# Moving the streamed operands of a matmul 16 bytes further down in SBUF

## The chip, the cores and the metric

The kernel runs on 1 core of a Trainium2 chip. The metric is the device time of one execution in microseconds, over several runs of the same kernel on the same chip.

## What is computed

The reference is a windowed attention with a few sink positions, followed by a feed-forward layer with a leaky rectifier. All data is float32.

```python
# attention: B, H, S, D = 4, 8, 768, 64; n_sink = 4; window = 128
scores = scale * np.matmul(q, k.transpose(0, 1, 3, 2))
keep = is_sink | in_window                  # in_window: 0 <= i - j < window
scores = np.where(keep, scores, -1000000000.0)
a = softmax(scores)
attn = np.matmul(a, v)
x = attn.transpose(0, 2, 1, 3).reshape(B * S, H * D)     # 3072 x 512
# feed-forward: d_model 512, d_ff 2048
h = x @ w_in
g = np.maximum(h, 0.0) + alpha * np.minimum(h, 0.0)
out = g @ w_out
```

## The kernel before

The 3072 rows of x are cut into 12 chunks of 256 query positions. For each chunk the kernel first does the attention of all 8 heads (scores, softmax, values), which leaves x transposed: four slices of 128 model dimensions by 256 positions. Then comes the feed-forward part, in 16 slices f of 128 hidden units. While TensorE does the feed-forward slices of chunk c, the attention of chunk c+1 is threaded between them.

To get float32 accuracy from the fast matmul, each operand is split into a high and a low part: x into `xh` and `xl`, g into `gh` and `gl`, and each weight into two parts in the tile `w{f}` (8192 bytes a partition: input and output weights, high and low). A product is then three matmuls: high by high, high by low, low by high.

The first product, `gemm1` (line 894), takes for each slice f twelve matmuls: four slices of the model dimension times three part pairs. The weights `w` are the stationary operand (128 columns are loaded for each matmul), and x is the moving operand, 256 columns of 4 bytes. ScalarE and VectorE then make g from the result (lines 898 to 901) and split it. The second product, `gemm2` (lines 929 to 932), takes six matmuls per slice f: here `gh` or `gl` is the stationary operand and the weights `w` stream, 512 columns.

The weights of all 16 slices stay in SBUF. They are loaded and split during the first two chunks.

The order of the work is written down in `program` as a list of operations with costs and needs; a planner (`Plan.draw`) plays them through and fixes, for each engine, one order and, for each rotating buffer, which copy is used. The planner's costs are constants: it does not know addresses. So the order of instructions does not depend on where a tile lies.

A tile has the same byte offset in all 128 partitions. The allocation puts tiles one after the other. In the kernel before, 15 of the 16 weight tiles start 32 bytes beyond a multiple of 128, and `w14` starts 64 beyond one, since it comes ahead of the others, behind a tile of 64 bytes. The tiles of `xh`, `xl`, `g`, `gh` and `gl` start 96 bytes beyond a multiple of 128. All of these tiles, and all slices that a matmul takes from them, are multiples of 128 bytes long, so that for every matmul of line 894 the moving operand lies 64 bytes beyond the stationary one, modulo 128 (32 for f=14). The two buffers `kq` of the scores (lines 597 and 598) start at 96 and at 0.

Of the kernel before, what the change touches and what calls it, by code (L numbers as in the profile page):

```python
# [10 lines left out]
F32R = mybir.dt.float32r  # L11
# [8 lines left out]
P = 128  # L20
# [4 lines left out]
QC = 2 * P  # L25
# [4 lines left out]
KT = DM // P  # L30
LAG = 2
# [290 lines left out]
def program(ctx, tc, qk, pairs, vp, vq, vs, w, par, out):  # L322
    nc = tc.nc
    const = ctx.enter_context(tc.tile_pool(name="const", bufs=1))
    fast = ctx.enter_context(ExitStack())
    pool = fast.enter_context(tc.tile_pool(name="main", bufs=1))
    psum = ctx.enter_context(tc.tile_pool(name="psum", bufs=1, space=bass.MemoryType.PSUM))
    plan = Plan(tc)
# [6 lines left out]
    def several(name, n, shape, dtype):  # L335
        plan.kind(name, [pool.tile(shape, dtype, name=f"{name}{i}") for i in range(n)])
# [17 lines left out]
    several("sinkT", 1, [P, QC], F32R)  # L354
    several("vs", 1, [P, DM], F32R)
    several("ob", 2, [P, DM], F32)
    several("xh", 2, [P, KT, QC], F32R)
    several("xl", 2, [P, KT, QC], F32R)
    several("g", 2, [P, QC], F32)
    several("gh", LAG + 1, [P, QC], F32R)  # L360
    several("gl", LAG + 1, [P, QC], F32R)

    size = const.tile([P, NF], F32, name="size")
    sizes = held(size)
# [182 lines left out]
    xh, xl, prep, comb, sink, ptile_, sums, rinv, nms, wt = {}, {}, {}, {}, {}, {}, {}, {}, {}, {}  # L547
# [730 lines left out]
```

## Time and profile before

| what | before |
| --- | --- |
| median of 3 runs | 677.37 us (676.48 to 678.82) |
| span of the profiled execution | 676.2 us |
| TensorE (PE) busy | 663.8 us, 98% |
| VectorE (DVE) busy | 525.8 us, 78% |
| ScalarE (ACT) busy | 397.5 us, 59% |
| granted TensorE clock, mean | 0.994 |

The profiled execution's span, 676.2 us, is the time from its first to its last instruction; it stands 1.2 us below the median of the timed runs. In the profile, PE is the matmul stream and PEld is the loading of stationary operands, which runs beside it. The duration of a matmul contains a tail that the profiler models; the time that a matmul really costs in a stream is the distance from its start to the next start. The names in a row are tiles: `bank<-xh,w` is a matmul into a PSUM bank with moving operand xh and stationary operand w; `bank<-w,gh` has the weights moving and gh stationary.

### The profile page before, as it was taken

The page shows a single profiled execution, that of the slowest core. Times are in us where ns is not written, and L with a number is a line of the kernel's source. Part 1 is how long each engine was busy: PE and PEld are TensorE (multiplying, and loading weights), DVE is VectorE, ACT ScalarE, POOL GpSimd, SP SyncE. Part 2 cuts the span into 40 slices and gives each one's busy share as a digit, 9 for nine tenths or more (in the row PEclk, how much of TensorE's full clock was granted, in tenths as well). Part 3 has the DMA queues.
Part 4 walks back from the last instruction along what each step waited for, and adds up shares of the span by engine and source line. Part 5 has one row for each costly group of instructions (what it writes and reads, how often), then busy time and mean ns, then how long its engine had stood idle before and what let it go on. Part 6 is the DMA issues. An engine that isn't in the chain of part 4 may idle for free.

```text
span 676.2 us, 13243 instructions
## 1 busy us (share of the span) xinstructions
PE 663.8 (98%) x4532; PEld 580.5 (86%) x4534; DVE 525.8 (78%) x1750; ACT 397.5 (59%) x1066; POOL 34.5 (5%) x115
## 2 busy tenths in 40 slices
PE   9989999999999999999999999999999999999996
PEld 4577898888989989989988988988998988998995
DVE  6999999968967976986986995995895994994331
ACT  6989888827636726736636735644744753853332
POOL 2110000001000000000000000010000000000000
PEclk9979999999999999999999999999999999999999
DMA  8684641424343453443443433552542543420001
GB/s 314 229 277 151 241 187 39 127 71 147 122 133 107 122 148 93 145 132 95 141 118 114 143 107 93 163 140 61 172 128 78 161 128 88 142 94 17 32 2 35
DMA packets 58683, 85.19 MB, mean 126 GB/s; under 512 B 9072, under 2 KB 35056, under 8 KB 58608
## 3 DMA queue, kind: packets, MB, share of 16 engines
q1 hardware_dynamic: 55056, 71.17, 34.7%
q10 hardware_dynamic: 3552, 13.11, 5.4%
q8 instruction: 37, 0.61, 0.4%
q14 instruction: 38, 0.31, 0.1%
HBM read 67.22 MB, written 17.04 MB: 125 GB/s over the span
## 4 chain that ended last, share of the span: by engine, by line
PE 83%; DVE 9%; ACT 5%; issue 2%; POOL 0%; DMA 0%; ACTq 0%; SPq 0%; POOLq 0%
PE bank L894 35%; PE bank L931 12%; PE bank L932 11%; PE bank L929 11%; PE bank L786 3%; PE bank L598 3%; PE bank L597 3%; PE bank L875 2%; DVE wa L396 2%; ACT pt L614 1%; ACT wa L382 1%; DVE wa L394 1%; DVE w L404 1%; DVE g L899 1%; DVE gl L901 1%
## 5 line engine op out<-in xcount | busy, mean ns | idle before, releaser
L894 PE MATMUL bank<-xh,w 128*128 128x256 f32 x1536 | 307.9, 283 | 0.4 <-DVE g L899 0.2
L894 PEld LDWEIGHTS bank<-xh,w 128*128 128x128 f32 x1536 | 250.6, 189 | 9.0 <-DVE g L899 3.0
L894 PE MATMUL bank<-xl,w 128*128 128x256 f32 x768 | 215.1, 280 | 0.1
L898 ACT ACTIVATE g<-bank,param 128x256 f32<-128x256 f32 x192 | 90.5, 472 | 117.4 <-PE bank L894 113.1
L931 PE MATMUL bank<-w,gh 128*128 128x512 f32 x382 | 151.7, 397 | 0.2 <-ACT gh L900 0.2
L932 PE MATMUL bank<-w,gh 128*128 128x512 f32 x382 | 150.1, 393 | 0.0
L894 PEld LDWEIGHTS bank<-xl,w 128*128 128x128 f32 x768 | 145.2, 189 | 4.4 <-DVE xl L808 0.3
L614 ACT ACTIVATE pt<-pt,nm 128x260 f32<-128x260 f32 (+1 forms) x192 | 94.5, 493 | 53.5 <-DVE nm L610 53.1
L899 DVE TENSOR_TENSOR g<-bank,g 128x256 f32<-128x256 f32 x192 | 79.7, 419 | 51.4 <-ACT g L898 50.9
L929 PE MATMUL bank<-w,gl 128*128 128x512 f32 x382 | 119.5, 394 | 0.0
L900 ACT CAST gh<-g 128x256 fp32r<-128x256 f32 x192 | 76.9, 404 | 59.7 <-DVE g L899 59.6
L901 DVE TENSOR_TENSOR gl<-g,gh 128x256 fp32r<-128x256 f32 x192 | 80.5, 423 | 26.5 <-ACT gh L900 23.0
L610 DVE CUSTOM_DVE_ANT_0 pt<-bank,masks 128x260 f32<-128x260 f32 (+1 forms) x192 | 75.0, 401 | 19.3 <-PE bank L598 15.5
L929 PEld LDWEIGHTS bank<-w,gl 128*128 128x128 f32 x382 | 70.7, 188 | 16.2 <-issue 0.7
L931 PEld LDWEIGHTS bank<-w,gh 128*128 128x128 f32 x382 | 71.9, 188 | 9.5 <-ACT gh L900 0.7
L932 PEld LDWEIGHTS bank<-w,gh 128*128 128x128 f32 x382 | 71.9, 188 | 8.3
L563 DVE TENSOR_TENSOR kq<-stage,kq 64x392 fp32r<-64x392 f32 x80 | 45.3, 566 | 2.7
L659 POOL TENSOR_TENSOR sink<-pt,ri 128x8 f32<-128x8 f32 x80 | 20.8, 264 | 504.7 <-DVE ri L644 358.8
L597 PE MATMUL bank<-kq 128*128 128x260 f32 (+1 forms) x160 | 44.4, 278 | 1.3 <-DVE nm L610 1.3
L598 PE MATMUL bank<-kq 128*128 128x260 f32 (+1 forms) x160 | 45.0, 281 | 0.0
L655 DVE CUSTOM_DVE_ANT_0 comb<-pt,ri 128x128 f32<-128x128 f32 x136 | 43.1, 343 | 0.4
L561 ACT CAST kq<-stage 128x392 fp32r<-128x392 f32 x80 | 40.9, 512 | 0.7 <-ACT pt L614 0.2
(130 smaller groups left out, 686.9 us busy)
## 6 DMA issues: line engine op xcount, KB each, us to landing
stage<-qk SPq DMA_DIRECT2D x80, 324.0 KB, 2.9
wraw<-w ACTq DMA_DIRECT2D x12, 1024.0 KB, 5.9
swap<-comb SPq DMA_DIRECT2D x36, 256.0 KB, 2.0
comb<-swap SPq DMA_DIRECT2D x36, 256.0 KB, 3.2
v<-vq SPq DMA_DIRECT2D x36, 192.0 KB, 2.5
out_dram<-ob SPq DMA_DIRECT2D x22, 256.0 KB, 3.5
wraw<-w SPq DMA_DIRECT2D x4, 1024.0 KB, 12.0
v<-vp SPq DMA_DIRECT2D x8, 192.0 KB, 6.9
```

The costliest lines, as they stand in the source:

```text
L597: nc.tensor.matmul(s[:, w0], qh()[:, qs], ks()[:, kw], start=True, stop=False)
L598: nc.tensor.matmul(s[:, w0], ql()[:, qs], ks()[:, kw], start=False, stop=True)
L610: op("DVE", dve(n), lambda: nc.vector.tensor_tensor_reduce(out=pt.at[:, u, w0], in0=s.at[:, w0], in1=masks[:, i, w0], scale=-0.125, scalar ...
L614: op("ACT", exp(n), lambda: nc.scalar.activation(pt.at[:, u, w0], pt.at[:, u, w0], AF.Exp, bias=nm.at[:, h, u:u + 1], scale=-1.0, accum_ou ...
L894: nc.tensor.matmul(h(), fin.at[:, 0, part, ks], rhs.at[:, kt], start=(kt == 0 and n == 0), stop=(kt == KT - 1 and n == 2))
L898: op("ACT", act(QC, True), lambda: nc.scalar.activation(g.at, h(), AF.Copy, scale=alt[:, f:f + 1]), reads=[bk, known("param")], writes=[g])
L899: op("DVE", dve(QC), lambda: nc.vector.tensor_tensor(g.at, h(), g.at, ALU.max), reads=[bk], writes=[g])
L900: op("ACT", cast(QC), lambda: nc.scalar.copy(gh.at, g.at), reads=[g], writes=[gh])
L901: op("DVE", dve(QC), lambda: nc.vector.tensor_tensor(gl.at, g.at, gh.at.bitcast(F32), ALU.subtract), reads=[g, gh], writes=[gl])
L929: nc.tensor.matmul(o2[j].at, gl.at[:, js], fin.at[:, 1, 0], start=False, stop=(f == NF - 1))
L931: nc.tensor.matmul(o2[j].at, gh.at[:, js], fin.at[:, 1, 0], start=(f == 0), stop=False)
L932: nc.tensor.matmul(o2[j].at, gh.at[:, js], fin.at[:, 1, 1], start=False, stop=False)
```

## The change

The four buffers of x and the six of gh and gl are no longer tiles of their own. They become slices of one tile, `operands`, that is 128 bytes longer than their sum, and the slices start 28 words (112 bytes) into it. That tile would start 96 bytes beyond a multiple of 128, so x, gh and gl now start at 96 + 112 = 208, which is 80 beyond one. x lies 48 bytes beyond the weights and no longer 64. The two buffers `g` are allocated ahead of it and stay at 96. The reserve for DMA descriptors at the bottom of SBUF is cut from 16384 to 8192 bytes, which makes room and moves everything down by a multiple of 128. No instruction is added, removed or moved in the order.

```diff
-    several("xh", 2, [P, KT, QC], F32R)
-    several("xl", 2, [P, KT, QC], F32R)
     several("g", 2, [P, QC], F32)
-    several("gh", LAG + 1, [P, QC], F32R)
-    several("gl", LAG + 1, [P, QC], F32R)
+    SHIFT = 28
+    reads_ = pool.tile([P, 4 * KT * QC + 2 * (LAG + 1) * QC + 32], F32R, name="operands")
+    place = lambda i, n: reads_[:, SHIFT + i * QC:SHIFT + (i + n) * QC]
+    xs = [place(i * KT, KT).rearrange("p (k q) -> p k q", k=KT) for i in range(4)]
+    plan.kind("xh", xs[:2])
+    plan.kind("xl", xs[2:])
+    plan.kind("gh", [place(4 * KT + i, 1) for i in range(LAG + 1)])
+    plan.kind("gl", [place(4 * KT + LAG + 1 + i, 1) for i in range(LAG + 1)])
...
-    nc = _bacc.Bacc("TRN2", target_bir_lowering=False, num_devices=1)
+    nc = _bacc.Bacc("TRN2", target_bir_lowering=False, num_devices=1, dynamic_dma_scratch_size=8192)
```

## The prediction

> **What bounds the kernel now.** I read the page first: the shares by engine, the chain of work that ended last, and the costliest groups.
>
> ```profile
> span 676.2 us, 13243 instructions
> PE 663.8 (98%) x4532; PEld 580.5 (86%) x4534; DVE 525.8 (78%) x1750; ACT 397.5 (59%) x1066; POOL 34.5 (5%) x115
> PE 83%; DVE 9%; ACT 5%; issue 2%; POOL 0%; DMA 0%; ACTq 0%; SPq 0%; POOLq 0%
> PE bank L894 35%; PE bank L931 12%; PE bank L932 11%; PE bank L929 11%; PE bank L786 3%; PE bank L598 3%; PE bank L597 3%; PE bank L875 2%; DVE wa L396 2%; ACT pt L614 1%; ACT wa L382 1%; DVE wa L394 1%; DVE w L404 1%; DVE g L899 1%; DVE gl L901 1%
> ```
>
> TensorE bounds it: 83% of the chain, and 69% (35+12+11+11) is the two products of the feed-forward part, lines 894 and 929 to 932. The table by stage says where a shorter matmul would reach the end (columns: length, then busy time and count of PE, PEld, DVE, ACT, POOL, then clock, DMA share, GB/s).
>
> ```profile
> 17.00:160.00 143.00, 137.92 (x921) 114.31 (x919) 131.86 (x331) 114.33 (x267) 10.32 (x22) 0.98 0.49 166
> 160.00:640.00 480.00, 479.82 (x3351) 431.92 (x3351) 373.87 (x1348) 262.85 (x748) 20.66 (x73) 1.00 0.39 116
> ```
>
> From 160 to 640 us PE is busy for 479.82 of 480 us at full clock, while DVE has 106 us of slack: each nanosecond off a matmul there is a nanosecond off the end. Before 160 us DVE (131.86 of 143) nearly ties with PE, so I count half of what is gained there. The groups of that middle stage, by line:
>
> ```profile
> L894 PE MATMUL bank<-xh,w 128*128 128x256 f32 x1179 | 233.3, 281 | 0.2 <-DVE g L899 0.2
> L894 PE MATMUL bank<-xl,w 128*128 128x256 f32 x589 | 164.4, 279 | 0.0
> L931 PE MATMUL bank<-w,gh 128*128 128x512 f32 x295 | 116.6, 395 | 0.0
> L932 PE MATMUL bank<-w,gh 128*128 128x512 f32 x296 | 116.3, 393 | 0.0
> L929 PE MATMUL bank<-w,gl 128*128 128x512 f32 x296 | 92.4, 393 | 0.0
> ```
>
> The mean (second number behind the bar) holds a fixed modelled tail, so I use it only for differences; the true price is the distance between starts. For that I read the timeline at single blocks: 12 matmuls of line 894 for one slice f, then the first of what follows.
>
> ```profile
> 345.52 0.28 PE L894 MATMUL bank<-xh,w 128*128 128x256 f32 x1
> ...
> 346.94 0.40 PE L931 MATMUL bank<-w,gh 128*128 128x512 f32 x1
> ...
> 357.33 0.28 PE L894 MATMUL bank<-xh,w 128*128 128x256 f32 x1
> ...
> 358.69 0.39 PE L931 MATMUL bank<-w,gh 128*128 128x512 f32 x1
> ```
>
> The same work, the same tiles, no wait: the block of f=12 takes 1.42 us (118 ns a matmul), that of f=15 takes 1.36 us (113 ns). By line, the two forms are these (a slow block, f=11, then the fast one):
>
> ```profile
> L894 PE MATMUL bank<-xh,w 128*128 128x256 f32 x6 | 1.1, 281 | 0.0
> L894 PE MATMUL bank<-xl,w 128*128 128x256 f32 x3 | 0.8, 281 | 0.0
> ...
> L894 PE MATMUL bank<-xh,w 128*128 128x256 f32 x7 | 1.3, 277 | 0.0
> L894 PE MATMUL bank<-xl,w 128*128 128x256 f32 x4 | 1.1, 276 | 0.0
> ```
>
> The stage mean of the xl matmuls, 279, lies three fifths of the way from 276 to 281: some 60% of the blocks run in the slow form. So there are about 0.06 us a block to be had or lost, and a block holds its form from matmul to matmul.
>
> **The change, part by part.** Instructions, their order and the queues stay. What moves are addresses. By the order of allocation, the weight tiles start 32 bytes beyond a multiple of 128, w14 alone at 64; x, gh and gl start at 96 now and at 80 afterwards. Every tile is a multiple of 128 bytes along the partition where it matters, so the difference (moving operand less weight operand, modulo 128) is the same for all matmuls of a line: for line 894 (x streams, w is loaded) 64 becomes 48, for f=14 it is 32 and becomes 16; for lines 929 to 932 (w streams, gh or gl is loaded) 64 becomes 80, for f=14 it is 96 and becomes 112. The difference between x and gh stays 0, because they move together.
>
> *Does the difference matter at all?* Slice 14 is a test that the kernel already holds. Its second product beside that of f=13 (first matmul, then the first of what follows six matmuls later):
>
> ```profile
> 358.69 0.39 PE L931 MATMUL bank<-w,gh 128*128 128x512 f32 x1
> ...
> 360.07 0.28 PE L894 MATMUL bank<-xh,w 128*128 128x256 f32 x1
> ...
> 361.45 0.40 PE L931 MATMUL bank<-w,gh 128*128 128x512 f32 x1
> ...
> 362.86 0.28 PE L597 MATMUL bank<-kq 128*128 128x260 f32 x1
> ```
>
> At 64 six matmuls take 1.38 us, at 96 they take 1.41 us. A second test is line 598, the last score matmul of a head: while it streams, the weights of the next matmul are loaded, and its own operand alternates between two tiles 32 bytes apart modulo 128. Four single instances, with the difference of its stream to the next weights: 16 (at 207.4 us), 48 (210.6), 64 (258.5) and 80 (100.2).
>
> ```profile
> L598 PE MATMUL bank<-kq 128*128 128x260 f32 x1 | 0.3, 284 | 0.0
> ...
> L598 PE MATMUL bank<-kq 128*128 128x260 f32 x1 | 0.3, 281 | 0.0
> ...
> L598 PE MATMUL bank<-kq 128*128 128x260 f32 x1 | 0.3, 283 | 0.0
> ...
> L598 PE MATMUL bank<-kq 128*128 128x260 f32 x1 | 0.3, 280 | 0.0
> ```
>
> The same instruction costs 3 ns more or less by where the next weights lie, and 48 and 80, the two differences that the change makes, are the cheap ones; 64, the present one, is 2 to 3 ns dearer. So the load of the next weights and the stream do disturb each other.
>
> The Trainium skill, "SBUF — State Buffer", section "SBUF: two separate sides", says otherwise: only the port pair that VectorE and GpSimd share causes contention on the engine side, and TensorE never waits for anyone. By that rule a shift of 16 bytes gives 677.4 us; the 1.38 against 1.41 us above do not fit it.
>
> *First product (line 894), 64 to 48.* The stage holds 1768 matmuls, 147 blocks. Bounds: all blocks fast saves 60% x 147 x 0.06 = 5.3 us; all slow costs 40% x 147 x 0.06 = 3.5 us. I take two thirds of the slow blocks turning fast, -3.5 us, because the row nearest to it (line 598 at 48) is on the cheap side.
>
> *Second product (lines 929 to 932), 64 to 80.* The stage holds 887 matmuls, 148 blocks of six. The row at 96 says +0.03 us a block, +4.4 us; line 598 at 80 says 3 ns a matmul less, -2.7 us. Since 80 lies midway between 64 and 96 and the two rows disagree, I take 0 and keep both ends.
>
> *The rest.* Some 45 blocks lie outside the stage; at the same price, 45 x 0.6 x 0.06 x 2/3 = 1.1 us, half of it on the path: -0.5 us. The f=14 blocks (10 of 147) go to differences 16 and 112; line 598 at 16 is 3 ns dearer than at 48, 12 x 10 x 3 ns = +0.4 us at most, inside the range. Line 598 meets gh at 64 and 32 instead of 48 and 16; by the rows +2 ns some 70 times, 0.1 us. VectorE and ScalarE read and write x and gh 16 bytes lower; they have slack in the middle stage, which covers it. Were that cover gone, 192 instructions of line 901 at, say, 10 ns each would be 2 us. The smaller reserve for descriptors shifts every tile by the same 8192 bytes, a multiple of 128, and no DMA is issued from GpSimd; I cost it at nothing.
>
> Sum: -3.5 + 0 - 0.5 = -4.0 us, against a span of 676.2: 672.2. The median of the runs, 677.37, lies 1.2 us above that span, which I add: 673.4 us. Late next would be the same waits that are there now (line 894 waits on DVE for g); as PE has next to no idle time in the middle stage, they swallow little.
>
> **Rivals.**
>
> *The second product pays (slower).* Place: the six matmuls of lines 929 to 932. If 80 behaves as 96 does, each block costs 0.03 us, +4.4 us in the stage and some +0.8 outside (45 x 0.03, about half counted); with the first product unchanged this gives 677.4 + 5.2 = 682.6 us. It decides as soon as the second product loses more than 3.5 us, that is 0.024 us a block. For it speaks the only long series at another difference in this trace; against it line 598 at 80.
>
> *Nothing changes.* The form of a block is set by how it is entered, and the two forms exist at the same addresses; a shift by 16 bytes may only redraw which blocks are slow. Then 677.4 us. For it: f=14 at difference 32 takes 1.41 us for its 12 matmuls, between the two forms:
>
> ```profile
> 351.58 0.28 PE L894 MATMUL bank<-xh,w 128*128 128x256 f32 x1
> ...
> 352.99 0.39 PE L931 MATMUL bank<-w,gh 128*128 128x512 f32 x1
> ```
>
> Against it: line 598, which is entered alike and still differs by address. The Trainium skill's rule quoted above, "SBUF — State Buffer", section "SBUF: two separate sides", would also come out here; this chance covers it.
>
> *Both gain.* All first-product blocks fast (-5.3, and -0.8 outside) and the second product at 3 ns less a matmul (-2.7, -0.4 outside): 677.4 - 9.2 = 668.2 us. For it: line 598 at 48 and at 80.
>
> **How the numbers follow.** Forecast 0.35, both gain 0.14, nothing changes 0.20, second product pays 0.31. Lowest bound 668.2, and a little lower if the fast form still has something in it: 667. Highest, all first-product blocks slow and the second like 96: 677.4 + 3.5 + 5.2 = 686; with 2 in 10 left out the range is 667 to 684. The likeliest case by itself spans 670 to 675. A measurement of this kernel tells about 0.3% (2 us) from no change. Faster 0.49, same 0.20, slower 0.31.
>
> **What would show it.** Right: in the middle stage the means of line 894 fall from 281/279 towards 277/276, blocks of 1.42 us become rare, lines 929 to 932 stay near 393 to 395, and the stretch ends some 4 us earlier with PE still fully busy. Wrong: means of lines 929 to 932 at 397 or more; line 894 at 281 or above in nearly all blocks; or both unchanged and the time too. If PE's groups shorten but PE shows idle time before them, the gain went into waits on DVE or ACT instead.

## The result and the profile after

The changed kernel takes 682.43 us (median of 4 runs, 681.95 to 682.94) against 676.96 us: a ratio of 1.0074, 95% interval 1.0056 to 1.0091. It is slower by 5.5 us.

The page of the changed kernel (span, engines, the chain by engine and by line; line numbers are 4 higher than before):

```profile
span 680.0 us, 13243 instructions
PE 667.8 (98%) x4532; PEld 584.1 (86%) x4534; DVE 526.1 (77%) x1750; ACT 399.4 (59%) x1066; POOL 35.0 (5%) x115
PE 89%; DVE 5%; ACT 4%; issue 1%; POOL 0%; ACTq 0%; POOLq 0%
PE bank L898 39%; PE bank L935 13%; PE bank L936 13%; PE bank L933 12%; PE bank L790 3%; PE bank L602 3%; PE bank L601 3%; PE bank L879 2%; ACT pt L618 1%; PE bank L1090 1%; DVE wa L400 1%; ACT wa L386 1%; PE bank L863 1%; DVE pt L614 1%; DVE w L408 1%
```

The same instructions, the same DVE time, 4 us more of PE, and PE's part of the chain grew from 83% to 89%. The table by stage and the groups of the middle stage:

```profile
160.00:640.00 480.00, 479.87 (x3321) 432.00 (x3320) 372.11 (x1339) 261.57 (x740) 20.85 (x73) 1.00 0.38 115
```
```profile
L898 PE MATMUL bank<-operands,w 128*128 128x256 f32 x1750 | 234.6, 282 | 0.1
L936 PE MATMUL bank<-w,operands 128*128 128x512 f32 x292 | 115.6, 396 | 0.0
L935 PE MATMUL bank<-w,operands 128*128 128x512 f32 x292 | 115.4, 395 | 0.0
L933 PE MATMUL bank<-w,operands 128*128 128x512 f32 x291 | 91.6, 396 | 0.0
```

PE is as full as before and at full clock, but in the same 480 us it gets through 1750 matmuls of the first product and not 1768, and through 875 of the second and not 887. At 118 and 233 ns each, these 30 missing matmuls are 4.9 us, about the whole loss of 5.5. (The two profiled spans, 676.2 and 680.0 us, lie only 3.8 apart; from 17 to 160 us the granted clock was 0.98 in the profile before and 1.00 in this one.) No new wait has come.

The timeline, at the block that was fast before (f=15, the first product's twelve matmuls, then the first of the second product):

```profile
357.85 1.59 PE L898 MATMUL bank<-operands,w 128*128 128x256 f32 x12
359.28 0.39 PE L935 MATMUL bank<-w,operands 128*128 128x512 f32 x1
```

From 357.85 to 359.28 it takes 1.43 us, where it took 1.36. Of the blocks of twelve in the middle stage that no other matmul interrupts, 62 of 139 took under 1.39 us before, the shortest 1.363; now none of 136 does, and the shortest takes 1.415. Counted by matmul, 687 of 1768 lay 113 or 114 ns before the next start in the kernel before, and 5 of 1747 do now. The fast form is gone.

The start times also show how a block comes to be fast. Leaving out the first and the last matmul of each block, 59 of the 139 blocks before stay above 115 ns throughout and 26 at 115 ns or less; 51 begin slow and change over to 113 or 114 ns on the way, and three mix. In none does a stretch of three fast matmuls turn slow again.

Below, "spacing" is the mean distance from one matmul's start to the next start in the middle stage, worked out from the start times of the trace. Slice 14, whose difference is another, is left out, and so are distances over 1.1 times the median (they contain waits). Before: 116.1 ns for the first product, 231.0 ns for the second, over 1633 and 823 matmuls; after: 118.3 and 232.9 ns.

### The profile page after: what moved, and what is told of

It is laid out like the page before. It is cut to its first block, busy times and chain, and to the rows that moved or that the text cites. A ratio compares the mean times of both kernels' runs of the same rounds, so it can differ in the third digit from the quotient of the medians.

```text
span 680.0 us, 13243 instructions
## 1 busy us (share of the span) xinstructions
PE 667.8 (98%) x4532; PEld 584.1 (86%) x4534; DVE 526.1 (77%) x1750; ACT 399.4 (59%) x1066; POOL 35.0 (5%) x115
## 4 chain that ended last, share of the span: by engine, by line
PE 89%; DVE 5%; ACT 4%; issue 1%; POOL 0%; ACTq 0%; POOLq 0%
PE bank L898 39%; PE bank L935 13%; PE bank L936 13%; PE bank L933 12%; PE bank L790 3%; PE bank L602 3%; PE bank L601 3%; PE bank L879 2%; ACT pt L618 1%; PE bank L1090 1%; DVE wa L400 1%; ACT wa L386 1%; PE bank L863 1%; DVE pt L614 1%; DVE w L408 1%
## 5 line engine op out<-in xcount | busy, mean ns | idle before, releaser
L898 PE MATMUL bank<-operands,w 128*128 128x256 f32 x2304 | 311.6, 283 | 0.4
L898 PEld LDWEIGHTS bank<-operands,w 128*128 128x128 f32 x2304 | 294.5, 188 | 13.2 <-DVE g L903 2.6
L935 PE MATMUL bank<-w,operands 128*128 128x512 f32 x382 | 151.7, 397 | 0.0
L936 PE MATMUL bank<-w,operands 128*128 128x512 f32 x382 | 151.1, 396 | 0.0
L933 PE MATMUL bank<-w,operands 128*128 128x512 f32 x382 | 120.4, 396 | 0.0
L904 ACT CAST operands<-g 128x256 fp32r<-128x256 f32 x192 | 77.0, 404 | 57.5 <-DVE g L903 57.3
L905 DVE TENSOR_TENSOR operands<-g,operands 128x256 fp32r<-128x256 f32 x192 | 80.3, 422 | 26.6 <-ACT operands L904 23.0
L933 PEld LDWEIGHTS bank<-w,operands 128*128 128x128 f32 x382 | 71.2, 189 | 16.2 <-issue 0.7
L935 PEld LDWEIGHTS bank<-w,operands 128*128 128x128 f32 x382 | 71.7, 188 | 9.6 <-ACT operands L904 0.8
L936 PEld LDWEIGHTS bank<-w,operands 128*128 128x128 f32 x382 | 72.2, 189 | 8.7
L618 ACT ACTIVATION_READ_ACCUMULATOR pt<-pt,nm 128x1 f32 x192 | 36.2, 189 | 0.0
L601 PEld LDWEIGHTS bank<-kq 128*128 128x128 f32 x160 | 30.2, 188 | 5.6 <-DVE nm L614 2.0
```

What stands on the lines that cost most here:

```text
L601: nc.tensor.matmul(s[:, w0], qh()[:, qs], ks()[:, kw], start=True, stop=False)
L618: op("ACT", exp(n), lambda: nc.scalar.activation(pt.at[:, u, w0], pt.at[:, u, w0], AF.Exp, bias=nm.at[:, h, u:u + 1], scale=-1.0, accum_ou ...
L898: nc.tensor.matmul(h(), fin.at[:, 0, part, ks], rhs.at[:, kt], start=(kt == 0 and n == 0), stop=(kt == KT - 1 and n == 2))
L904: op("ACT", cast(QC), lambda: nc.scalar.copy(gh.at, g.at), reads=[g], writes=[gh])
L905: op("DVE", dve(QC), lambda: nc.vector.tensor_tensor(gl.at, g.at, gh.at.bitcast(F32), ALU.subtract), reads=[g, gh], writes=[gl])
L933: nc.tensor.matmul(o2[j].at, gl.at[:, js], fin.at[:, 1, 0], start=False, stop=(f == NF - 1))
```

## The experiments

All experiments start from the changed kernel, with two tiles in place of one, so that x (28 words or another number) and gh/gl can be placed apart; three have the weights 28, 4 or 1 words into longer tiles as well, and three change the load. A longer weight tile is 8320 bytes and not 8192, so there neighbouring weight tiles do not start at the same place modulo 256. The common edit:

```diff
-    reads_ = pool.tile([P, 4 * KT * QC + 2 * (LAG + 1) * QC + 32], F32R, name="operands")
+    xall = pool.tile([P, 4 * KT * QC + 32], F32R, name="opx")            # x at XSHIFT
+    gall = pool.tile([P, 2 * (LAG + 1) * QC + 32], F32R, name="opg")     # gh, gl at GSHIFT
...
-            fin.at = const.tile([P, 2, 2, DM], F32R, tag=f"w{f}", name=f"w{f}")
+            fin.at = const.tile([P, 4 * DM + 32], F32R, tag=f"w{f}", name=f"w{f}")[:, WSHIFT:WSHIFT + 4 * DM]...
```

The two theories after the result: A, the difference between the streamed and the stationary operand sets the spacing; B, the place of x and gh by itself sets it. C stands for everything else in the edit.

### What carries the loss, and whether it is the difference

**Put back to 96, rest of the edit kept** (`XSHIFT, GSHIFT, WSHIFT = 0, 0, 0`).

> x, gh and gl as slices of larger tiles and the smaller descriptor reserve, as in the changed kernel, but put back at 96 beyond a multiple of 128 (difference 64). Theory A (the difference between streamed and stationary operand sets the matmul's spacing): 677 us, line of the first product at 116.1 ns a matmul in the middle stage, second at 231.0. Theory B (the absolute place of x and gh, 80 against 96, sets it): the same, 677. Theory C (the place does not matter; the merged tiles or the smaller reserve do): 682 us, 118.3 and 232.9 ns.

**Only x at 80** (`28, 0, 0`).

> Only x moves to 80 (difference 48 in the first product); gh and gl stay at 96. Theories A and B: the first product goes to 118.3 ns, the second stays at 231.0; 2304 x 2.2 ns = 5.1 us, of which the saturated stage passes on all and the rest half: 681 to 682 us. Rival (the second product carries the loss, as my slower rival had it): 677 to 678.

**Only gh and gl at 80** (`0, 28, 0`).

> Only gh and gl move to 80 (difference 80 in the second product); x stays at 96. Theories A and B: the second product goes from 231.0 to 232.9 ns, 1152 x 1.9 = 2.2 us at most, 678 to 679 us; the first stays at 116.1 with its two forms. My slower rival of the prediction: the whole 5 us lies here, 682.

**Everything 16 down, the weights too** (`28, 28, 28`).

> x, gh, gl and the weights all move down by 16 modulo 128: x at 80 as in the changed kernel, but the difference back at 64. Theory A: 677 us, 116.1 and 231.0 ns, with the two forms of 113 and 118. Theory B: 682 us, 118.3 and 232.9 ns.

**Only the weights, 16 up** (`0, 0, 4`).

> x, gh and gl stay at 96 beyond a multiple of 128; the weights move up by 16 instead, to 48 (w14 to 80). The differences are those of the changed kernel, 48 and 80. Theory A (difference): 682 us, the first product at 118.3 ns without the fast form. Theory B (place of x): 677 us, 116.1 ns.

The first product's group in the middle stage, in the order above (count and mean; in 480 full us a larger count is a faster kernel):

```profile
L899 PE MATMUL bank<-opx,w 128*128 128x256 f32 x1771 | 233.5, 280 | 0.2 <-DVE g L904 0.2
```
```profile
L899 PE MATMUL bank<-opx,w 128*128 128x256 f32 x1752 | 235.0, 282 | 0.1
```
```profile
L899 PE MATMUL bank<-opx,w 128*128 128x256 f32 x1776 | 234.5, 281 | 0.2 <-DVE g L904 0.2
```
```profile
L899 PE MATMUL bank<-opx,w 128*128 128x256 f32 x1772 | 234.7, 280 | 0.3 <-DVE g L904 0.3
```
```profile
L899 PE MATMUL bank<-opx,w 128*128 128x256 f32 x1755 | 234.5, 281 | 0.2 <-DVE g L904 0.2
```

Each ratio is to runs of the kernel before that were taken together with that row's runs; the medians of those runs lie between 676.96 and 677.99 us.

| kernel | difference, first / second product | time, us | ratio to before (95%) | spacing, ns | blocks under 1.39 us |
| --- | --- | --- | --- | --- | --- |
| before | 64 / 64 | 676.96 | 1 | 116.1 / 231.0 | 62 of 139 |
| after | 48 / 80 | 682.43 | 1.0074 (1.0056 to 1.0091) | 118.3 / 232.9 | 0 of 136 |
| put back | 64 / 64 | 678.42 | 1.0003 (0.9990 to 1.0016) | 116.1 / 232.0 | 56 of 138 |
| only x | 48 / 64 | 682.33 | 1.0074 (1.0048 to 1.0100) | 118.4 / 232.3 | 0 of 137 |
| only gh, gl | 64 / 80 | 676.92 | 0.9995 (0.9980 to 1.0010) | 116.3 / 231.0 | 48 of 138 |
| all moved | 64 / 64 | 677.58 | 1.0002 (0.9987 to 1.0018) | 116.4 / 230.0 | 52 of 138 |
| only weights | 48 / 80 | 681.26 | 1.0037 (1.0022 to 1.0051) | 117.9 / 231.8 | 0 of 138 |

Putting x back restores the time, so the merged tile and the smaller reserve cost nothing (C falls). Moving x alone gives the whole loss; moving gh and gl alone gives none. With everything moved x lies at 80, as in the slow kernel, and the time is that of before: the place of x by itself is not the cause (B falls). Moving only the weights, with x untouched, takes the fast form away just as well. So the difference between x and w decides, in these kernels, whether the fast form exists.

It is not the only thing: at the same difference of 48 the kernel with moved weights loses 0.4% and the changed one 0.7%, with a spacing of 117.9 against 118.3. (Their intervals do not overlap; against that of "only x", 1.0048 to 1.0100, they do.) The trace shows how it is spread. With moved weights the spacing goes by slice: 116.6 to 117.7 ns for f = 2, 4, 6, 8, 10, 12, 13 and 15, and 118.6 to 119.4 for f = 0, 1, 3, 5, 7, 9 and 11. The weight tiles of the first group start at 176 modulo 256, those of the second at 48, since tiles 8320 bytes apart alternate. In the kernel with only x moved, where all weight tiles but w14 start at 32 modulo 256, the slices lie between 118.1 and 119.2. So in this kernel the difference modulo 128 is not the whole address that counts. The difference modulo 256 does not settle it either: it is 48 in the first group, as in the changed kernel (118.3). No run here takes the larger distances apart.

Two expectations missed in size: the second product did not answer to its difference (231.0 at 80 with gh alone, expected 232.9), and it changes by 2 ns (230.0 to 232.3) between kernels in which its difference is 64.

### The other differences

x, gh and gl together at `4, 8, 12` and `16` words, the weights in place:

> x, gh and gl 16 bytes further up instead of down: difference 80 in the first product, 48 in the second. Theory A1 (the spacing repeats with 64 bytes and rises towards 32, symmetrically): like 48, 118.3 ns in the first product, 682 us. Theory A2 (48 is a bad place and its mirror is a good one): 113.5 to 115 ns, 670 to 674 us.

> Difference 96 in the first product, 32 in the second. A1 (repeats with 64 bytes): the first product like slice 14 of the kernel before at 32, 117.2 ns, 679 to 680 us. If the period is 128 bytes instead, no row gives the value; by the score matmuls (283 against 281 of the modelled mean) dearer than 48, over 118.3 ns and 683 us or more.

> Difference 112 in the first product, 16 in the second. A1 (period of 64 bytes): as at 48, 118.3 ns, 682 us. Without that period: slice 14 of the changed kernel, at 16, has 118.7 ns, which bounds it from nearby: 117 to 119 ns, 679 to 684 us.

> Difference 0 in both products. A1 (period of 64 bytes): as the kernel before, both forms of 113 and 118 ns, mean 116.1, 677 us. Rival (streamed and stationary operand in the same place of every 128 bytes is the worst case): over 119 ns in the first product, 685 us or more.

The first product's group in the middle stage for differences 80, 96, 112 and 0:

```profile
L899 PE MATMUL bank<-opx,w 128*128 128x256 f32 x1751 | 235.6, 283 | 0.1
```
```profile
L899 PE MATMUL bank<-opx,w 128*128 128x256 f32 x1752 | 234.4, 282 | 0.2 <-DVE g L904 0.2
```
```profile
L899 PE MATMUL bank<-opx,w 128*128 128x256 f32 x1760 | 234.4, 281 | 0.2 <-DVE g L904 0.2
```
```profile
L899 PE MATMUL bank<-opx,w 128*128 128x256 f32 x1745 | 235.2, 283 | 0.1
```

| difference, first / second | time, us | ratio | spacing, ns |
| --- | --- | --- | --- |
| 80 / 48 | 683.70 | 1.0073 (1.0050 to 1.0095) | 118.9 / 232.3 |
| 96 / 32 | 683.04 | 1.0072 (1.0039 to 1.0104) | 118.1 / 233.7 |
| 112 / 16 | 680.53 | 1.0045 (1.0030 to 1.0060) | 117.3 / 232.2 |
| 0 / 0 | 683.46 | 1.0077 (1.0054 to 1.0101) | 119.0 / 232.1 |

A period of 64 bytes is refuted: 0 is among the worst (119.0), 64 is the best. The step to 96 missed both of its prices: the time is that of the dearer one (683.04 us), the spacing that of neither. The two remaining steps are known from slice 14 alone: 117.1 ns at 32 (the kernel before; 116.8 to 118.2 in the three others with this difference), 118.7 at 16 (the changed one). Of the six steps run with all slices, 64 is the only one with blocks under 1.39 us, and the kernel before stood on it. The second product stays within 230 to 234 ns in all runs so far.

### Steps smaller than 16 bytes

x alone 4 bytes up, 4 down, 8 up (`XSHIFT` 1, 31, 2):

> x 4 bytes further up than in the kernel before: difference 68; gh and gl stay at 96. If the unit that counts is 16 bytes, x now straddles it: the first product between 116.1 (64) and 118.9 ns (80), 677 to 683 us. If a small lead turns all blocks to the fast form: 113.4 ns, 670 to 672 us.

> x 4 bytes further down than in the kernel before: difference 60; gh and gl at 96. Between 64 and 48: 116.1 to 118.3 ns, 677 to 682 us. All blocks fast: 113.4 ns, 670 to 672 us.

> x 8 bytes further up: difference 72; gh and gl at 96. Halfway between 64 (116.1) and 80 (118.9): 117.5 ns, 680 us, if the spacing changes evenly; 118.9 ns, 683 us, if only the exact 64 has the fast form; 113.4 ns, 671 us, if all blocks turn fast.

```profile
L899 PE MATMUL bank<-opx,w 128*128 128x256 f32 x1728 | 236.7, 285 | 0.1
```
```profile
L899 PE MATMUL bank<-opx,w 128*128 128x256 f32 x1760 | 234.0, 280 | 0.2 <-DVE g L904 0.2
```
```profile
L899 PE MATMUL bank<-opx,w 128*128 128x256 f32 x1728 | 235.8, 285 | 0.1
```

At 68 the kernel takes 689.42 us (1.0162, 1.0140 to 1.0185; 121.3 ns), at 60 680.73 us (1.0038, 1.0022 to 1.0055; 117.3 ns), at 72 687.84 us (1.0139, 1.0117 to 1.0162; 120.9 ns). The hope for a place where all blocks are fast failed. 68 and 72 are worse than either of their neighbours, 64 and 80, and above every time expected for them (683 us at most); this points to another effect, which the next runs take apart.

### Is it the load beside the stream?

The first asks whether the difference alone rules: all operands, the weights too, 4 bytes up (`1, 1, 1`). In the other three the load of the first product does not walk through SBUF, while x lies at 96, 80 and 100:

```diff
-                nc.tensor.matmul(h(), fin.at[:, 0, part, ks], rhs.at[:, kt], ...
+                nc.tensor.matmul(h(), fin.at[:, 0, part, kt * P:kt * P + 1].broadcast_to([P, P]), rhs.at[:, kt], ...
```

> x, gh, gl and the weights all 4 bytes up: difference 64 as in the kernel before, but nothing starts at a multiple of 16 bytes. Difference alone counts: 677 us, 116.1 ns in the first product. The straddling of 16 bytes by x counts by itself: 688 to 690 us, 121.3 ns, as with x alone 4 bytes up.

> The first product loads one weight column 128 times instead of 128 columns (it leaves out the other weights of w_in; its sums are other numbers); x at 96, as before. If the load's walk through SBUF disturbs the stream: the slow form goes, 113 ns or less in all blocks, 116.1 - 113.3 = 2.8 ns x 2304 = 6 us less, 670 to 672 us, and below that if part of the 113 was disturbance too (the bf16 filler matmuls take 217 ns for 512 columns, 108.5 for 256). If not: 677 us, both forms.

> The same with x at 80 (before the load stood still: 118.3 ns, 682 us). Load disturbs: the spacing equals that of the kernel with x at 96 and one column. Place of x by itself: 2 ns above it, 118 ns.

> The same with x at 100 (before: 121.3 ns, 689 us). Load disturbs: the spacing equals that at 96. Place of x by itself: some 5 ns above it.

The groups of the middle stage, first all 4 bytes up (both products), then the standing load with x at 96, 80 and 100:

```profile
L899 PE MATMUL bank<-opx,w 128*128 128x256 f32 x1720 | 234.3, 284 | 0.0
L937 PE MATMUL bank<-w,opg 128*128 128x512 f32 x286 | 114.5, 400 | 0.0
```
```profile
L899 PE MATMUL bank<-opx,w 128*128 128x256 f32 x1773 | 232.0, 279 | 0.2 <-DVE g L904 0.2
```
```profile
L899 PE MATMUL bank<-opx,w 128*128 128x256 f32 x1776 | 231.5, 278 | 0.2 <-DVE g L904 0.2
```
```profile
L899 PE MATMUL bank<-opx,w 128*128 128x256 f32 x1738 | 235.8, 283 | 0.1
```

| kernel | time, us | ratio | spacing, ns |
| --- | --- | --- | --- |
| all 4 bytes up | 692.10 | 1.0204 (1.0174 to 1.0233) | 120.8 / 237.3 |
| standing load, x at 96 | 675.75 | 0.9971 (0.9952 to 0.9989) | 115.2 / 232.1 |
| standing load, x at 80 | 675.65 | 0.9980 (0.9946 to 1.0014) | 114.5 / 233.0 |
| standing load, x at 100 | 686.29 | 1.0118 (1.0089 to 1.0147) | 120.0 / 233.2 |

With the load standing still, x at 80 costs no more than x at 96 (114.5 and 115.2 ns; 112 of 139 and 102 of 138 blocks under 1.39 us): the 2 ns between 48 and 64 need a load that walks. That is theory A with its mechanism, the stream of one matmul disturbed by the load that runs beside it. In the profile before, that is the load for the following matmul: the one for the matmul that starts at 304.00 us starts at 303.88. What the two reads clash in is not shown. But x at 100 stays slow, 120.0 ns, with the load standing, and a difference of 64 does not help when everything starts 4 bytes off (120.8; here the second product, whose streamed weights are now off too, goes to 237.3). So starting the stream 4 bytes beyond a multiple of 16 costs by itself, some 5 ns in 256 columns (120.0 against 115.2). Not every odd start does: 60, which is 12 bytes beyond one, takes 117.3 with the load walking. It is a second effect that the change, which moves by 16, does not touch. With everything 4 bytes off the time, 692.10 us, is above the 688 to 690 expected, since the second product pays too. My expectation that the slow form would vanish wholly with a standing load was too strong: with x at 96 and at 80, 1039 of 1771 and 1283 of 1774 matmuls are at 113 or 114 ns, against 687 of 1768 before. No form faster than 113 appeared.

## Why the prediction was wrong

*What bounds.* Right. PE is full in the middle stage, a nanosecond there reaches the end, and 30 matmuls missing from that stage make up 4.9 of the 5.5 us lost.

*Two forms of a block, and some 60% slow.* Right in number: 687 of 1768 matmuls were at 113 or 114 ns. Not right is that a block holds its form: 51 of 139 blocks begin slow and change over to the fast form. That addresses decide was right too.

*The first product, 64 to 48.* This step failed, in its sign: -3.5 us predicted. It is x alone that gives the whole loss, 1.0074. The spacing of the first product rose by 2.2 ns; times the 1768 matmuls of the stage this is 3.9 us, where my bound for "all slow" was +3.5. (The second product's 1.9 ns, times 887, are another 1.7 us in the changed kernel's profile.) The fault lies in the row that I took as nearest, single matmuls of line 598. Its price is steady in the kernel before: ahead of the second product, in the middle stage, 31 of 34 take 284 ns with one buffer `kq` and 31 of 35 take 280 with the other. But the price does not follow from the difference alone. Between the kernel put back and the one with only x moved, neither the stream of this matmul (line 603 there) nor the gh that is loaded beside it changes place; yet with the first buffer all 34 go from 282 or 283 ns to between 287 and 289. The price of a matmul of another line did not carry over to long runs of line 894, where what counts is whether the fast form can set in and last. Of the steps run, it does at 64 alone. A better row stood in the prediction: the block of f=14 at difference 32, with twelve matmuls. I read its 1.41 us as lying between two forms and filed it under "nothing changes", when its matmuls, at 113 to 120 ns by turns, show no stretch of the fast form at all. I also asked only which share of slow blocks a shift might heal, and took the fast form for a property of the block that would stay available.

*The second product, 64 to 80: 0.* Nearly right; alone it does nothing (0.9995), though the changed kernel shows 232.9 against 231.0 there. The row of f=14 at 96 (234.3 ns) did not carry over to 80.

*The rival that came true in time* (682.6 us) came true for another reason: it put the loss into lines 929 to 932, and the run with only gh and gl moved shows that none of it lies there. "All first-product blocks slow" stood only as an end of the range, without a rival of its own; it is what happened.

*Nothing changes.* Refuted, and with it the rule of the Trainium skill ("SBUF — State Buffer", section "SBUF: two separate sides") that TensorE never waits on anyone there, if it is read to cover TensorE's own two reads: with the instructions and their order unchanged, the place of the weights moves the time by 0.4%, and of x by 0.7%.

*The rest.* The merged tile and the smaller reserve, put at nothing: right, 1.0003. *Late next:* right, PE stayed full and no new wait came.

## What to carry to other kernels

Where matmuls follow each other without a gap, the byte offset of the streamed operand relative to the stationary one is worth 1 to 2.5% of their spacing here (116.1 ns against 117.3 to 119.0), so read the distance of starts before and after anything that moves tiles, an added small tile included. Judge a place by long runs of matmuls at that place; a single matmul of another line can point the wrong way. Start streamed operands at a multiple of 16 bytes (4 and 8 beyond one took 121 ns), and where PE is full, try the few offsets on the chip, since no row of another place gave the value.

## What the runs showed of the hardware that was not expected

- The same matmul of 256 float32r columns takes 113 or 118 ns in long runs at the same addresses, with what goes before it: in the kernel before, slice f=9 runs at 113 ns in six of nine chunks, and at 117 to 120 throughout in the three where its first matmul takes 166. A run can go over from the slow form to 113, as 51 of 139 blocks do. With the streamed operand 64 bytes beyond the stationary one both forms occur, at 48, 80, 96, 112, 0 and 60 none of the blocks was under 1.39 us.
- A stream that starts 4 or 8 bytes beyond a multiple of 16 takes 121 ns, at 4 bytes also with the load beside it standing still (120.0); 12 bytes beyond costs 117.3, no more than some multiples of 16 do.
- Places of operands that a matmul does not touch can show in it: the last score matmul ahead of the second product goes, with one of its buffers, from 282 or 283 ns to between 287 and 289 when x alone moves, although neither it nor the load beside it reads x.
- No place was found that beats the kernel before. By spacing it stands on the best of the six steps of 16 bytes that were run, and slice 14 at the other two was slower; the steps are counted modulo 128, and the kernel with moved weights (116.6 to 117.7 ns and 118.6 to 119.4, by weight tile) shows that its spacing goes with where a tile lies modulo 256.
